# Another order of the same instructions in a fused attention and feed-forward kernel

## The chip, the cores and the metric

The kernel runs on one core of a Trainium2 chip. The metric is the time that the device takes for one execution, in microseconds (us); lower is better. A core has five engines with an instruction stream each: TensorE (PE, matrix products; its weight loads are shown apart as PEld), VectorE (DVE), ScalarE (ACT), GpSimd (POOL) and SyncE (SP), which here only issues transfers. Each engine takes its own instructions strictly in the order in which they stand, and waits at an instruction until the semaphores that it names have been raised by other engines or by transfers that have landed.

## What is computed

Attention of 8 batches x 8 heads over 576 queries of 64 elements, with keys and values averaged over groups of 8 (72 keys are left), and behind it a gated feed-forward layer on the 4608 tokens of 512 elements:

```python
k_p = k.reshape(B, H, Sp, pool, D).mean(axis=3)      # pool = 8, Sp = 72
v_p = v.reshape(B, H, Sp, pool, D).mean(axis=3)
scores = scale * np.matmul(q, k_p.transpose(0, 1, 3, 2))
attn = softmax(scores)                                # written out in the reference
x = np.matmul(attn, v_p)                              # as (4608, 512)
gate = 1.0 / (1.0 + np.exp(-(x @ w_gate)))            # w_gate, w_val: 512 x 1536
return (gate * (x @ w_val)) @ w_out                   # w_out: 1536 x 512
```

## The kernel before

**Tiles.** The 4608 tokens are nine blocks of 512. The first block is worked through by `first_pass` (L1147) in a hand-written list of steps, `ORDER` (L65). The other eight follow in four rounds of two blocks: `hidden_second` (L961) or `hidden` (L989) for the products with the gate and value weights, and `second_sums` (L1069) for those with the output weights. Between the products of a round stand the steps of the attention of the blocks that come next (`attention`, L722), as generators that are advanced a step at a time.

**Products.** A float32 product is made of three PE products of rounded numbers: every operand is split into a high part (a cast on ACT, `split`, L365) and the low rest (a subtraction on DVE). In the names, `hs` and `oparts` are such pairs of the hidden values and of the output weights, `parts` those of the gate and value weights, `xo` those of the attention's result. PE writes `chain` (gate and value products) and `acc` (output products), each in matmuls with 512 columns. For a pair of blocks the products are of sums and differences of quarters, seven in place of eight.

**Weights.** They arrive as 64-bit numbers and become float32 on the chip, in `to_f32` (L384): for each piece of 128x1024 elements two ACT instructions (`w<-raw` and `raw<-raw,cst`), one min/max and one shift-and-or on DVE or POOL, and behind these the split into parts. This falls into the first 150 us or so; later rounds read back the parts, which are kept in HBM (`kept...`). The rows call the loaded pieces `raw` (`raw64_...` and `raw_o_...` in the lists of instructions) and the converted ones `w` and `w_o`. The attention's steps show as `sc` (scores), `tp` and `tr` (transposes through PE), `av` (product with the values), `early`, `e`, `pm`, `ph`, `pl`, `r`, `rest`, `vres`, `vr`.

**What sets the order.** Nothing is issued while these functions run. Every engine call is taken down in a book (`Book`, `Taken`, `Engine`, L273 to L326), a group of matmuls as one unit, and at the end the units are issued in the order of a table:

```python
with tc.manual_schedule(engines={e.engine for e in engines}):
    for n in LATER.split() or range(len(book.units)):
        for taken in book.units[int(n)]:
            taken.issue(link)
```

`LATER` (L112 to L268) has 3801 numbers, one for each unit. So the table sets the order on every engine; which instruction waits for which follows from the data and the buffers. The call that is taken down is made in L317, which is why every row of the profile names that line. SP's transfers go round eight semaphores: the ninth is issued only when the first has landed, the tenth when the second has, and so on.

Of the kernel before, what the change touches and what calls it, by code (L numbers as in the profile page):

```python
# [112 lines left out]
5 4 3 6 0 10 2 7 24 13 17 19 20 8 26 12 27 18 16 30 9 22 21 75 25 34 36 35 46 32 1 44 39 54 38 40 11 29 47 28 51 15 31  # L113
65 52 66 37 61 57 41 67 62 42 14 60 63 53 73 82 45 74 70 87 79 71 97 136 84 123 77 112 109 111 80 88 100 99 101 96 98
59 83 104 91 105 89 81 106 72 130 78 107 110 93 92 95 94 58 114 127 115 116 119 125 86 103 120 128 197 144 122 143 142
135 141 85 137 138 129 157 205 140 147 145 121 102 204 134 132 153 154 152 133 155 151 131 222 90 108 139 118 161 203
164 149 124 162 148 216 126 163 156 167 150 166 189 170 158 169 174 159 165 146 171 190 160 55 168 177 179 243 172 173
117 178 56 193 180 186 230 181 223 182 199 244 233 201 196 206 200 202 209 185 184 33 188 225 192 49 191 176 195 240
175 236 183 187 234 226 247 239 238 250 245 251 259 217 248 257 282 253 242 258 212 279 283 64 276 252 232 261 286 267
237 43 269 211 278 50 256 274 219 268 254 218 277 266 265 231 275 272 241 280 221 299 288 298 284 228 305 227 229 285  # L120
289 292 113 302 290 281 293 255 235 273 294 303 316 300 246 326 332 329 304 333 335 301 311 287 318 331 330 328 327
317 334 307 308 306 198 309 314 352 322 260 312 315 325 362 324 353 208 364 291 345 323 366 339 313 346 348 338 365
349 321 340 296 399 350 360 310 215 376 68 342 405 361 341 297 358 343 214 344 69 367 347 295 263 382 355 373 370 337
264 374 380 224 375 270 271 377 336 371 386 387 356 385 354 395 357 372 398 396 397 393 411 392 403 402 48 207 368 391
400 412 363 417 406 410 407 369 419 378 404 409 401 388 418 416 389 408 414 413 424 426 320 447 319 425 23 423 381 427
422 262 379 446 429 420 384 434 421 383 194 444 430 220 457 437 435 431 578 466 436 483 441 485 443 452 449 451 492
210 428 469 470 467 468 464 461 493 462 213 463 450 432 433 497 486 500 390 440 487 415 501 448 438 456 584 471 484
472 480 498 481 477 490 439 458 473 517 482 502 249 478 479 460 521 513 465 474 491 475 499 530 454 453 531 590 488
532 527 476 510 522 489 524 528 394 525 445 523 685 529 504 526 507 495 540 546 496 516 545 505 459 519 506 514 494
455 511 534 442 544 533 542 512 503 577 541 551 548 520 582 535 556 518 549 557 558 76 596 567 560 568 570 571 536 569  # L130
611 564 543 603 574 572 550 580 606 581 351 565 515 555 566 561 554 612 562 539 573 604 576 607 632 563 605 597 600
579 598 552 583 608 538 601 537 602 599 648 622 623 559 642 629 553 627 669 359 678 636 575 628 672 953 659 656 675
588 591 679 613 585 633 586 676 667 660 593 595 594 589 680 666 587 592 673 614 677 609 670 610 621 508 674 615 630
# [1436 lines left out]
```

## Time and profile before

| what | us |
|---|---|
| three runs | 906.82, 908.58, 909.71 |
| their median | 908.58 |
| the profiled execution, its own time | 906.58 |
| span of its trace | 904.8 |
| PE busy | 891.4 |
| PE's weight loads busy | 732.7 |
| DVE busy | 657.4 |
| ACT busy | 544.5 |
| POOL busy | 200.0 |

The span is from the first to the last record of the profiled execution; 1.8 us of the own time lie outside of it. Busy times are sums over one engine. The granted clock of PE is at 1.00, that is the 2.4 GHz level, in every stretch that is shown.

### The profile page before, as it was taken

The numbers are of one execution on the slowest core, as the hardware profiler recorded it, in microseconds if no ns is written. First come the engines' busy times: TensorE is split into PE (matmuls) and PEld (weight loads), VectorE is DVE, ScalarE is ACT, GpSimd is POOL, SyncE is SP. The second block draws the span as 40 slices with busy tenths as digits, with TensorE's granted clock in tenths as the row PEclk, the third lists the DMA queues.
The fourth block names the chain that finished last, engine by engine and source line by source line (L and its number), as shares of the span: only waits on it lengthen the run. The fifth ranks groups of instructions, "written<-read, shape, count | busy, mean of one in ns | idle before, by whom it ended". The sixth has DMA issues, their size and how long they took to land.

```text
span 904.8 us, 12625 instructions
## 1 busy us (share of the span) xinstructions
PE 891.4 (99%) x4148; PEld 732.7 (81%) x4148; DVE 657.4 (73%) x1038; ACT 544.5 (60%) x1110; POOL 200.0 (22%) x369
## 2 busy tenths in 40 slices
PE   6999999999999999999999999999999999999998
PEld 5788878888888888888888888888888888888886
DVE  7989888889899999756668796355589552224863
ACT  5998998788978476545375555445365552224352
POOL 2422101012164235443443104132213000000000
PEclk9999999999999999999999999999999999999999
DMA  9899888889999888787987877676747776645554
GB/s 337 309 326 336 301 335 298 298 285 338 320 324 316 276 287 286 237 299 259 308 276 237 244 273 264 229 268 194 264 122 252 245 249 207 228 167 204 192 169 143
DMA packets 100433, 237.56 MB, mean 263 GB/s; under 512 B 13872, under 2 KB 34992, under 8 KB 98832
## 3 DMA queue, kind: packets, MB, share of 16 engines
q1 hardware_dynamic: 85328, 203.97, 66.6%
q0 software_dynamic: 15040, 32.79, 10.4%
q8 instruction: 33, 0.54, 0.2%
q14 instruction: 32, 0.26, 0.1%
HBM read 176.02 MB, written 60.69 MB: 262 GB/s over the span
## 4 chain that ended last, share of the span: by engine, by line
PE 81%; ACT 2%; DVE 1%; issue 0%; ACTq 0%
PE chain L317 50%; PE acc L317 25%; PE av L317 3%; PE sc L317 3%; ACT hs L317 0%; DVE s L317 0%; DVE hs L317 0%; PE tp L317 0%; DVE h L317 0%; ACT e L317 0%; ACT L317 0%; ACT raw_o L317 0%; DVE w_o L317 0%; ACT w_o L317 0%; ACT oparts L317 0%
## 5 line engine op out<-in xcount | busy, mean ns | idle before, releaser
L317 PE MATMUL chain<-xo,parts 128*128 128x512 f32 x2316 | 544.1, 392 | 0.5 <-ACT xs L317 0.5
L317 PEld LDWEIGHTS chain<-xo,parts 128*128 128x128 f32 x2316 | 430.7, 188 | 93.3 <-issue 1.0
L317 PE MATMUL acc<-hs,oparts 128*128 128x512 f32 x1008 | 237.0, 391 | 0.2 <-issue 0.2
L317 PEld LDWEIGHTS acc<-hs,oparts 128*128 128x128 f32 x1008 | 188.1, 188 | 40.6 <-DVE hs L317 1.2
L317 POOL DMA_DIRECT2D turned<-turn x240 | 131.7, 551 | 214.3 <-DVE turn L317 184.3
L317 DVE TENSOR_TENSOR y<-chain,sV 128x512 f32<-128x512 f32 x46 | 31.1, 686 | 69.6 <-PE chain L317 54.7
L317 ACT CAST hs<-h 128x1024 fp32r<-128x1024 f32 x52 | 54.3, 1051 | 27.2 <-PE acc L317 22.4
L317 DVE TENSOR_TENSOR hs<-h,hs 128x1024 fp32r<-128x1024 f32 x52 | 63.0, 1217 | 10.5 <-ACT hs L317 10.3
L317 ACT COPY chain<-chain 128x512 f32<-128x512 f32 x46 | 26.5, 577 | 52.8 <-PE chain L317 45.8
L317 DVE TENSOR_TENSOR y<-chain,sG 128x512 f32<-128x512 f32 x46 | 31.2, 682 | 34.2 <-PE chain L317 23.4
L317 ACT CAST hs<-s 128x1024 fp32r<-128x1024 f32 x36 | 37.5, 1050 | 28.5 <-DVE s L317 13.0
L317 DVE TENSOR_TENSOR hs<-s,hs 128x1024 fp32r<-128x1024 f32 x36 | 43.8, 1218 | 11.1 <-ACT hs L317 10.9
L317 ACT COPY sG<-chain 128x512 f32<-128x512 f32 x46 | 26.6, 584 | 41.0 <-PE chain L317 39.4
L317 ACT ACT_TABLE_LOAD x37 | 47.5, 1283 | 0.6
L317 ACT COPY sV<-chain 128x512 f32<-128x512 f32 x46 | 26.7, 584 | 34.0 <-PE chain L317 32.7
L317 ACT ACTIVATE gate<-chain 128x512 f32<-128x512 f32 x46 | 26.9, 594 | 31.8 <-PE chain L317 29.4
L317 DVE TENSOR_TENSOR h<-chain,gate 128x512 f32<-128x512 f32 x46 | 30.7, 679 | 20.1 <-PE chain L317 20.0
L317 PE MATMUL sc<-kbd,raw 128*128 128x144 f32 (+1 forms) x262 | 41.4, 297 | 0.3 <-ACT pr L317 0.2
L317 PEld LDWEIGHTS sc<-kbd,raw 128*128 128x128 f32 (+1 forms) x262 | 33.5, 176 | 8.6 <-issue 2.8
L317 ACT ACTIVATE gate<-y 128x512 f32<-128x512 f32 x46 | 28.9, 632 | 17.0 <-DVE y L317 16.8
L317 PE MATMUL acc<-oparts,hs 128*128 128x512 f32 x144 | 38.7, 402 | 0.0
L317 DVE TENSOR_REDUCE m<-sc 128x4 f32<-128x288 f32 x48 | 21.7, 452 | 17.5 <-PE sc L317 17.2
(210 smaller groups left out, 1099.9 us busy)
## 6 DMA issues: line engine op xcount, KB each, us to landing
oparts<-keptS SPq DMA_DIRECT2D x48, 512.0 KB, 4.7
oparts<-keptO SPq DMA_DIRECT2D x72, 256.0 KB, 4.7
raw<-in_wgv SPq DMA_DIRECT2D x12, 1024.0 KB, 8.1
out<-o SPq DMA_DIRECT2D x34, 256.0 KB, 3.8
raw<-in_kT SPq DMA_DIRECT2D x28, 288.0 KB, 5.0
raw<-in_qT SPq DMA_DIRECT2D x29, 256.0 KB, 4.9
raw<-in_vm SPq DMA_DIRECT2D x24, 256.0 KB, 5.5
raw_o<-in_wo SPq DMA_DIRECT2D x12, 512.0 KB, 8.5
```

Of the source, the lines that this page charges most:

```text
L317: return self._book.take(lambda: f(*args, **named))
```

## The change

`LATER` is replaced by another table with the same 3801 numbers, and nothing else. 3675 units stand at another place, by 16.7 places in the mean and by 245 at most. The 6909 instructions of the program are the same, one for one; on each of the five engines they come in another order.

```diff
--- before.py
+++ after.py
@@ -110,161 +110,161 @@
 LATER = """
-5 4 3 6 0 10 2 7 24 13 17 19 20 8 26 12 27 18 16 30 9 22 21 75 25 34 36 35 46 32 1 44 39 54 38 40 11 29 47 28 51 15 31
...
+5 3 4 0 10 6 2 17 7 13 19 24 8 20 12 16 26 27 9 30 36 1 75 18 34 46 35 40 21 22 29 39 47 38 54 25 28 44 65 32 31 52 66
...
```

The lists below give, for one engine and one place, the instructions in their order (engine line, operation, what is written and read, with the number of the buffer, and the size).

**The start.** SP before, from its second row on: `in_qT` and `in_kT` are queries and keys, `in_wgv` the gate and value weights (1 MB a load), `early_217<-in_qT` the queries of the fourth pair of heads.

```order
L317 DMA h_216<-in_qT 128x512
L317 DMA h_216<-in_kT 128x576
L317 DMA cst_84<-in_const 128x133
L317 DMA h_216<-in_qT 128x512
L317 DMA h_216<-in_kT 128x576
L317 DMA h_216<-in_qT 128x512
L317 DMA early_217<-in_qT 128x512
L317 DMA xs0_220<-in_sums8 128x360
L317 DMA xs0_220<-in_vn 64x512
L317 DMA raw64_237<-in_wgv 128x2048
```

SP now:

```order
L317 DMA h_216<-in_qT 128x512
L317 DMA h_216<-in_kT 128x576
L317 DMA cst_84<-in_const 128x133
L317 DMA h_216<-in_qT 128x512
L317 DMA h_216<-in_kT 128x576 x2
L317 DMA xs0_220<-in_vn 64x512
L317 DMA h_216<-in_qT 128x512
L317 DMA xs0_220<-in_sums8 128x360
L317 DMA raw64_237<-in_wgv 128x2048
L317 DMA early_217<-in_qT 128x512
```

The first load of queries has moved ahead of one of keys, and that of the fourth pair's queries behind the first load of weights; the first twelve loads are the same twelve.

DVE before, at about 20 us: `early_218<-early_217,early_218` and `r3_261` lead to the first block's attention result `xo1_268`; `raw_236` and `raw_234` are keys of the next block.

```order
L317 TENSOR_TENSOR early_218<-early_217,early_218 128x512
L317 CAST r3_261<-rest_260 128x4x32
L317 TENSOR_REDUCE early_218<-raw_236 128x72
L317 TENSOR_TENSOR early_218<-early_217,early_218 128x512
L317 TENSOR_TENSOR vres1_105<-vr_248,vres1_105 32x128
L317 TENSOR_TENSOR r3_261<-rest_260,r3_261 128x4x32
L317 SCALAR_TENSOR_TENSOR w4_249<-w4_249,raw64_237 128x1024
L317 TENSOR_TENSOR vres3_107<-vr_248,vres3_107 32x128
L317 CAST parts_259<-w4_249 128x2x256
L317 TENSOR_TENSOR xo1_268<-av_267,xo1_268 128x512
L317 TENSOR_TENSOR vres2_106<-vr_248,vres2_106 32x128
L317 CAST parts_262<-w4_249 128x2x256
```

DVE now:

```order
L317 TENSOR_TENSOR early_218<-early_217,early_218 128x512
L317 CAST r3_261<-rest_260 128x4x32
L317 TENSOR_TENSOR early_218<-early_217,early_218 128x512
L317 TENSOR_TENSOR r3_261<-rest_260,r3_261 128x4x32
L317 TENSOR_REDUCE early_218<-raw_236 128x72
L317 TENSOR_TENSOR vres0_104<-vr_248,vres0_104 32x128
L317 SCALAR_TENSOR_TENSOR w4_249<-w4_249,raw64_237 128x1024
L317 TENSOR_TENSOR vres2_106<-vr_248,vres2_106 32x128
L317 CAST parts_259<-w4_249 128x2x256
L317 TENSOR_TENSOR xo1_268<-av_267,xo1_268 128x512
L317 TENSOR_REDUCE early_218<-raw_234 128x72
L317 TENSOR_TENSOR xo1_268<-av_264,xo1_268 128x512
```

The reduction of `raw_236` has moved behind both steps of `early_218` and `r3_261`; that of `raw_234` stands between the two `xo1_268` now, and a cast of weights (`parts_262`) behind them.

**At about 74 us.** ACT before: `xs0_220<-av_330` is the copy that empties a PSUM bank of the attention; `raw64_...`, `w4_...` and `parts_...` belong to the conversion of weights.

```order
L317 CAST parts_329<-w4_319 128x2x256
L317 ACTIVATE raw64_257<-raw64_257,cst_84 128x1024
L317 ACT_TABLE_LOAD
L317 ACTIVATE y_331<-chain_326 128x512
L317 CAST parts_320<-w4_285 128x2x256
L317 ACTIVATE w4_342<-raw64_328 128x1024
L317 ACTIVATE raw64_328<-raw64_328,cst_84 128x1024
L317 COPY xs0_220<-av_330 128x512
```

ACT now:

```order
L317 ACT_TABLE_LOAD
L317 ACTIVATE y_331<-chain_326 128x512
L317 ACTIVATE raw64_257<-raw64_257,cst_84 128x1024
L317 COPY xs0_220<-av_330 128x512
L317 ACTIVATE w4_342<-raw64_328 128x1024
L317 CAST parts_320<-w4_285 128x2x256
L317 ACTIVATE raw64_328<-raw64_328,cst_84 128x1024
```

Between `y_331` and the copy of `av_330` there stood a cast and two conversion steps; now one conversion step stands there. In the same way, at about 123 us, ACT's order was two conversion steps, a table load, `y_390`, two casts and `y_388`; it is now the table load, `y_388`, two conversion steps and `y_390`, and the PE transposes there no longer have an ACT instruction to wait for.

**At about 80 to 87 us.** PE before, from the first output products of the first block on: `pl_227` is the low part of the attention weights.

```order
L317 MATMUL acc<-oparts,hs 128x512 x24
L317 MATMUL av<-early 128x64
L317 MATMUL av<-other,vres_106 128x64
L317 MATMUL av<-ph,vh_95 128x448
L317 MATMUL av<-pl,vh_95 128x448
```

PE now:

```order
L317 MATMUL acc<-oparts,hs 128x512 x23
L317 MATMUL tr<-identr,r_335 96x128 x4
L317 MATMUL acc<-oparts,hs 128x512
L317 MATMUL av<-ph,vh_95 128x448
L317 MATMUL av<-pl,vh_95 128x448
```

`av<-pl` follows the output products in both, with four transposes ahead of the last of these now. The first of the 24 that waits for the low part of `oparts_338` is the sixth before and the eighth now. DVE before, from the low part of `oparts_338` to the conversion of the next output weights `w_o_349`:

```order
L317 TENSOR_TENSOR oparts_338<-w_o_333,oparts_338 128x2x512
L317 TENSOR_TENSOR pl_227<-tp_343,ph_226 128x448
L317 TENSOR_TENSOR parts_348<-w4_342,parts_348 128x2x256
L317 TENSOR_REDUCE early_218<-raw_234 128x72
L317 TENSOR_TENSOR vl1_100<-early_218,vh1_95 64x64 x2
L317 TENSOR_TENSOR other_223<-early_218,other_223 32x64
L317 TENSOR_SCALAR w_o_349<-w_o_349 128x1024
L317 TENSOR_REDUCE early_218<-raws_228 128x64
L317 TENSOR_REDUCE early_218<-raw_231 96x64
L317 TENSOR_TENSOR h_216<-chain_339,y_352 128x512
L317 TENSOR_REDUCE early_218<-raw_235 128x72
L317 SCALAR_TENSOR_TENSOR w_o_349<-w_o_349,raw_o_337 128x1024
```

DVE now:

```order
L317 TENSOR_TENSOR oparts_338<-w_o_333,oparts_338 128x2x512
L317 TENSOR_REDUCE early_218<-early_218 96x64
L317 TENSOR_SCALAR w_o_349<-w_o_349 128x1024
L317 TENSOR_REDUCE early_218<-raw_234 128x72
L317 SCALAR_TENSOR_TENSOR w_o_349<-w_o_349,raw_o_337 128x1024
L317 TENSOR_REDUCE early_218<-raw_233 128x64
L317 TENSOR_TENSOR pl_227<-tp_343,ph_226 128x448
```

Two steps of the conversion of `w_o_349` and three reductions stand between `oparts_338` and `pl_227` now, where there was nothing.

## Rows read from the trace of the kernel before

**Rows 1.** The profile page: the span, the busy time of each engine with its share of the span and its instructions, and the shares of engines in the chain that ended last.

```profile
span 904.8 us, 12625 instructions
PE 891.4 (99%) x4148; PEld 732.7 (81%) x4148; DVE 657.4 (73%) x1038; ACT 544.5 (60%) x1110; POOL 200.0 (22%) x369
...
PE 81%; ACT 2%; DVE 1%; issue 0%; ACTq 0%
```

**Rows 2.** The view of waits for PE: what it waited for, us in total, times, longest.

```profile
PE sc L317 <- DMA h<-in_qT: 5.5, 1, 5.5
PE tp L317 <- DVE early L317: 0.9, 1, 0.9
PE tp L317 <- DVE r L317: 0.6, 1, 0.6
PE tp L317 <- ACT y L317: 0.5, 1, 0.5
PE chain L317 <- ACT xs L317: 0.5, 1, 0.5
PE sc L317 <- issue: 0.2, 1, 0.2
PE vr L317 <- DMA xs<-in_vn: 0.2, 1, 0.2
PE tr L317 <- ACT early L317: 0.2, 1, 0.2
PE sc L317 <- ACT pr L317: 0.2, 1, 0.2
PE acc L317 <- issue: 0.2, 1, 0.2
```

**Rows 3.** Windows of 20 us, three early and one late: length, then busy us (and instructions) of PE, PEld, DVE, ACT, POOL, the granted clock of PE, the busy share of the DMA engines and GB/s.

```profile
40.00:60.00 20.00, 20.00 (x105) 16.29 (x104) 18.57 (x34) 19.89 (x58) 3.15 (x6) 1.00 0.99 331
60.00:80.00 20.00, 19.50 (x99) 15.90 (x98) 17.02 (x31) 19.44 (x46) 3.09 (x3) 1.00 1.00 371
80.00:100.00 20.00, 20.00 (x98) 16.90 (x97) 17.66 (x27) 16.92 (x43) 5.05 (x9) 1.00 0.81 275
```

**Rows 4.** The same view, one window of the last round.

```profile
760.00:780.00 20.00, 20.00 (x89) 16.38 (x88) 5.16 (x8) 5.65 (x11) 0.00 (x0) 1.00 0.71 238
```

**Rows 5.** The chain of work that ended last, its end: start, us, what.

```profile
859.96 32.19 PE acc L317 x142
...
900.76 0.37 ACT o L317
```

**Rows 6.** The timeline from 0 to 28 us: start, us, engine, operation, count, and in brackets the idle time before and what ended it. SPq is the issue of transfers.

```profile
1.66 0.42 SPq L317 DMA_DIRECT2D h<-in_qT  x1
...
5.51 4.33 PE L317 MATMUL sc<-kbd,h 128*128 128x144 f32 x16 [5.51 <-DMA h<-in_qT]
...
12.43 1.60 PE L317 MATMUL sc<-kbd,early 128*128 128x144 f32 x8
...
13.62 0.34 SPq L317 DMA_DIRECT2D raws<-in_vr  x1
...
14.95 0.55 PE L317 MATMUL tp<-cst,early 128*128 128x128 f32 x3 [0.91 <-DVE early L317]
...
20.56 0.74 DVE L317 TENSOR_REDUCE early<-raw 128x72 f32<-128x576 f32 x1
...
20.66 0.63 PE L317 MATMUL tp<-cst,early 128*128 128x128 f32 x4 [0.56 <-DVE r L317]
...
27.52 4.85 PE L317 MATMUL chain<-xo,parts 128*128 128x512 f32 x20
```

**Rows 7.** The timeline at 74 us.

```profile
72.35 1.22 ACT L317 ACTIVATE raw<-raw,cst 128x1024 uint32<-128x1024 uint16 x1
...
73.48 0.56 ACT L317 COPY xs<-av 128x512 f32<-128x512 f32 x1
...
74.09 1.20 PE L317 MATMUL chain<-xo,parts 128*128 128x512 f32 x4 [0.50 <-ACT xs L317]
```

**Rows 8.** The timeline of PE at 123 us.

```profile
123.69 0.66 PE L317 MATMUL tp<-cst,early 128*128 128x128 f32 x4 [0.54 <-ACT y L317]
```

**Rows 9.** The timeline of PE from 80 us.

```profile
80.44 5.64 PE L317 MATMUL acc<-oparts,hs 128*128 128x512 f32 x24
...
86.45 0.37 PE L317 MATMUL av<-pl,vh 128*128 128x448 f32 x1
```

**Rows 10.** The timeline of DVE in the same stretch.

```profile
80.14 1.23 DVE L317 TENSOR_TENSOR oparts<-w_o,oparts 128x1024 fp32r<-128x1024 f32 x1
81.28 0.62 DVE L317 TENSOR_TENSOR pl<-tp,ph 128x448 fp32r<-128x448 f32 x1
...
82.42 0.74 DVE L317 TENSOR_REDUCE early<-raw 128x72 f32<-128x576 f32 x1
...
84.28 0.69 DVE L317 TENSOR_SCALAR w_o<-w_o 128x1024 f32<-128x1024 f32 x1 [0.38 <-ACT w_o L317]
84.89 0.68 DVE L317 TENSOR_REDUCE early<-raws 128x64 f32<-128x512 f32 x1
85.48 0.67 DVE L317 TENSOR_REDUCE early<-raw 96x64 f32<-96x512 f32 x1
...
87.33 1.21 DVE L317 SCALAR_TENSOR_TENSOR w_o<-w_o,raw_o 128x1024 uint32<-128x1024 uint32 x1
```

308 rows, old and new, of the table LATER are left out of this document.

## The prediction

> **What bounds the kernel now.** I read the page first, then the waits of PE, then windows, and last the timeline at the few places where PE waits. The page says that PE is busy 891.4 of 904.8 us and stands for 81% of the chain that ended last, where ACT has 2% and DVE 1% [rows 1]. PE's whole list of waits holds 9.2 us, and 5.5 of them are the wait for the first queries, before anything can run [rows 2]. After 12 us only small ones are left: 0.9 and 0.6 for DVE in the attention of the first block, 0.5 and 0.5 for ACT at 74 and 123 us, and some of 0.2. No wait for a transfer comes after 11.4 us. So an order can win little: the 13.4 us in which PE is idle, less 5.5 of first load and 0.4 of the last copy [rows 5], leave 7.5 us, of which the list names 3.7. It can lose much more, since every wait that it makes on PE is added to the time.
>
> Where it may lose shows in the windows. In the last round ACT and DVE are busy 5 to 6 of 20 us [rows 4]; between 40 and 100 us, where the weights are converted, ACT is busy 16.9 to 19.9, DVE 17.0 to 18.6, and the DMA engines up to 1.00 [rows 3]. There PE, ACT, DVE and the transfers are all near full, and whatever stands ahead of a copy or cast that PE needs can stop PE. The end is a plain run of output products, 142 in 32.19 us, which is 0.2267 us a matmul [rows 5]; I use this pitch below. The granted clock is 1.00, the 2.4 GHz level, in all these windows, so nothing is to be had from the clock.
>
> **The change part by part.** No instruction is added or removed, so all busy sums stay and only waits can change. I work against the profiled execution, 906.58 us; the median of the three runs is 908.58, that is 2.0 more, and the difference that the change makes is put onto the median at the end. The runs spread by 0.3%, and about 0.3% (2.7 us) is what a measurement of this kernel can tell from no change.
>
> *The start.* The load of queries that ends PE's first wait was SP's third, issued at 1.66 for 0.42 us [rows 6], and is now its second: PE begins 0.4 us sooner. The fourth pair's queries were ninth and are now twelfth, right behind a 1 MB load. Since the ring of eight lets the twentieth load go when the twelfth has landed, the twentieth row of SP (`raws<-in_vr`, issued at 13.62 [rows 6]) tells when the twelfth landed; the first twelve are the same twelve, so the queries now land near 13.6. PE took them at 12.43 without waiting, in 1.60 us [rows 6]. So PE stalls 1.2 us there and is done by 15.2, but its next step waited until 14.95 for DVE anyway, 0.91 us of it idle [rows 6]: some 0.3 us of the 1.2 is left over. If that cover is gone, all 1.2 are lost. On DVE a reduction of 0.74 us has moved from ahead of the two steps that lead to the first block's result to behind them; the wait of 0.56 us that ends at 20.66 beside it [rows 6] can go. In sum −0.4 + 0.3 − 0.6 = −0.7. Ends: −1.9 if all three idle pieces (0.4, 0.9, 0.6) go, +0.8 if the queries cost 1.2 in full and only the 0.4 is won. I take −0.7, since each of its terms has a row. What is won shows in the start of the first long chain, 27.52 now [rows 6].
>
> The Trainium skill (DMA: Bandwidth & Descriptors, Anatomy of one DMA) gives a transfer about 2.0 us and its bytes at 436 GB/s; it measured that on GpSimd's queue, and these are SP's. By it the queries would land near 7.0 + 2.0 + 3.0 = 12.0 us, an estimate, and PE would not stall: the start would be worth −1.0 and not −0.7. The trace disagrees with it (13.62), and I go by the trace.
>
> *At 74 us.* PE waited 0.50 us for the copy that empties a bank; the copy began at 73.48, as soon as a conversion step of 1.22 us was through [rows 7]. Both steps of that piece stand behind the copy now, and only one other step stands between the activation and the copy. The wait goes: −0.5. Next late is the cast of weights behind it, which moved back by one conversion step; it is part of the term on what comes back.
>
> *At 123 us.* PE's transposes waited 0.54 us for an ACT activation behind a table load and two conversion steps [rows 8]; this activation now stands ahead of the conversion: −0.5. The activation behind it takes over a later place, but its product is read by matmuls further on.
>
> *What comes back.* With ACT at 19.9 and 19.4 of 20 us [rows 3], PE runs as fast as ACT lets it in this stretch. A microsecond that is won ahead of it does not make ACT's work any shorter. I put half of the 1.7 us won down as lost again: +0.85. The bounds are 0 and +1.7.
>
> *A new tight place at 80 to 87 us.* Before, DVE made the low part of the attention weights (`pl`) right behind the low part of the output weights, at 81.28 for 0.62 us [rows 10], and PE read it at 86.45 [rows 9], with 4.5 us to spare. Now five steps stand between: 0.67 + 0.69 + 0.74 + 1.21 + 0.68 and the 0.62 of `pl` itself make 4.61 us by the rows of their kind [rows 10], and since each begins some 0.08 us before the one ahead has ended (1.14 from start to start for 1.23), it is about 4.1. On PE's side, from the matmul that waits for the output weights on, 17 of the 24 are left, 17 × 0.2267 = 3.85 us, and four transposes of a quarter of the columns, some 0.06 each: 4.1 as well. The spare time has gone from 4.5 to about nothing. DVE had 0.2 us in hand at the start of this stretch (the low part was through at 81.37, and the sixth matmul came at 80.44 + 5 × 0.2267 = 81.57), and has two more matmuls in hand now. The price lies between 0 and 1.0 (DVE a microsecond late); I take +0.3, nearer to the lower end, because of these two matmuls.
>
> *Elsewhere.* In the two orders I counted the matmul groups whose operand comes from an ACT or DVE instruction that itself waits for a matmul fewer than nine matmuls earlier (2 us): 77 before, 94 now. 17 more short leads, most of them after 300 us, where ACT and DVE have room [rows 4]: 0 taken, up to 17 × 0.2 = 3.4 us if each costs what the small waits cost [rows 2]. Against them stand the four waits of 0.2 us for ACT or for nothing named [rows 2], which may go: −0.8 at best, 0 taken.
>
> Sum: −0.7 − 1.0 + 0.85 + 0.3 = −0.55, that is 906.0 for the profiled execution and 908.0 on the scale of the median.
>
> **The rivals.**
>
> *Faster by more.* ACT and DVE do not hold PE back, and the short leads hold. Then the start gives 1.9, the two ACT waits 1.0 and the two waits of 0.2 for ACT 0.4: −3.3, 905.3. For it: at the four largest waits of today behind the first one, what PE waits for now stands earlier on its engine. Against it: the shares of ACT [rows 3], and the late queries.
>
> *Slower.* One mechanism: conversion steps, of 1.2 us each [rows 7, 10], stand right ahead of the cast or copy for which PE waits, as at 74 us before. The new order puts more of them there: at 80 to 87 us (+1.0), and at the 17 short leads, 0.2 each (+3.4); the late queries add 0.8, and the two waits that go give 1.0 back: +4.2, 912.8. It decides from about a dozen of the 17 on being late. For it: the full engines between 40 and 100 us. Against it: most of the new short leads lie where ACT is busy a third of the time.
>
> *PE has room that its busy share hides.* PE's weight loads are busy 732.7 us, 81% [rows 1]; if the other 172 us were gaps that an order can close, the time could fall as far as 734.5. But in the late window without any wait the loads are busy 16.38 of 20 us [rows 4], 82%: this is what they show when PE is full, and 732.7 / 16.38 × 20 = 894.6 us is the floor. I give it 1 in 100. The rule behind it is the Trainium skill's (Perfetto Trace Analysis, Identifying the Most-Contended Engine), which takes the matmul's busy share for a bad measure and wants that of the loads; here the trace shows that both are full together.
>
> *Nothing moves.* If the moves only swapped instructions that wait for the same thing, the waits would stay and the time be 908.6. The lists of all five engines differ, also at the places at which PE waits, so 1 in 100.
>
> **How the numbers follow.** The forecast (908.0) has 0.58, the faster rival 0.22, the slower one 0.18, the last two 0.01 each. Of the forecast's 0.58, with its terms between −0.3 and +3 at their ends, 0.05 falls below 905.9 (faster by 0.3%), 0.03 above 911.3 and 0.50 between. The faster rival's own time lies just beyond the line: 0.18 faster, 0.04 same. The slower one: 0.16 slower, 0.02 same. Together with the last two: faster 0.24, same 0.57, slower 0.19. The range goes down to 903.8, past the faster rival by the part of the named waits that would be left, and up to 912.0, which leaves out the upper half of the slower rival; some 0.17 is outside.
>
> **What would show it right or wrong.** In the profile after: PE's first wait at 5.1 instead of 5.5; a wait for the fourth pair's queries near 12 us (wrong if there is none); the wait of 0.6 at 20 us gone and the first long chain at about 26.8; no wait of PE for ACT at 74 and 123 us; at about 86 us none or a short one for `pl`. The busy sum of PE's loads stays at 733. The last run of output products keeps its 0.2267 us. The prediction is wrong if PE's list holds several new waits of 0.2 us or more between 40 and 600 us (slower), or if the chain of waits is PE alone from 27 us on with the start 1.9 us sooner (faster). A wait of PE for a transfer after 30 us would be something that none of these cases has.

## The result, and the profile after

The changed kernel takes 916.86 us (median of four runs, 914.67 to 917.82) against 907.80 (906.82 to 909.71) of the kernel before, four runs as well: 9.1 us more, ratio 1.0094, interval 1.0068 to 1.0120. It is slower by 0.9%, beyond what the runs scatter by, and above 912.0, the upper end of the range. The profiled execution took 916.85 us, 10.27 more than that of before, with a span of 915.1.

The page after: span, busy time of each engine, and the shares of the chain that ended last.

```profile
span 915.1 us, 12653 instructions
PE 899.4 (98%) x4148; PEld 736.8 (81%) x4148; DVE 656.4 (72%) x1038; ACT 543.9 (59%) x1110; POOL 203.4 (22%) x369
...
PE 74%; DVE 6%; ACT 5%; DMA 2%; issue 1%; DVEq 0%; ACTq 0%
```

Beside [rows 1] one sees at once that this is not a matter of waits alone. The same 4148 matmuls are busy 8.0 us longer and their loads 4.1; PE's idle time has grown by 2.3 only, from 13.4 to 15.7. POOL is busy 3.4 us longer with its same instructions; DVE and ACT are not. So matmuls ran slower somewhere, and something on GpSimd took longer.

PE's waits after, in the columns of [rows 2]:

```profile
PE sc L317 <- ACT kbd L317: 5.6, 2, 5.2
PE sc L317 <- POOL kbd L317: 1.9, 1, 1.9
PE acc L317 <- DMA oparts<-keptS: 1.1, 1, 1.1
PE sc L317 <- issue: 0.6, 1, 0.6
PE chain L317 <- ACT chain L317: 0.5, 1, 0.5
PE sc L317 <- ACT e L317: 0.4, 2, 0.2
```

The waits that the prediction meant to remove are shorter or gone: the first is 5.2 long and not 5.5, and of DVE at 15 and 20 us (0.9, 0.6) and ACT at 74 and 123 us (0.5, 0.5) nothing is left. In their place stand three of 0.4 to 0.6 in the first 16 us, one of 1.9 for GpSimd (`kbd`, the pooled keys that are put in place for the scores) and one of 1.1 for a transfer.

**Where the loss falls.** I laid the two traces over each other by the columns that PE had worked through (the columns of its matmuls, added up). The changed kernel is 3.4 us behind when the other is at 40 us, 2.9 at 80 us, 6.9 at 92, 7.5 at 116, 7.8 at 266, 9.4 at 345, and 10.3 from 700 us on. So there are three pieces: the start, a place at 90 us that costs 4.0, and small losses later, 2.5 of them after 266 us.

*The start.* The windows from 0 to the first long chain of products, after and then before (columns as in [rows 3]):

```profile
0.00:30.68 30.68, 24.06 (x103) 19.09 (x103) 21.95 (x51) 16.65 (x37) 8.57 (x27) 1.00 0.88 315
```

```profile
0.00:27.52 27.52, 19.99 (x103) 15.35 (x103) 21.96 (x50) 16.53 (x36) 7.57 (x27) 1.00 0.95 347
```

Both hold the same 103 matmuls. PE's idle time has shrunk, from 7.53 to 6.62; but the matmuls themselves took 4.07 us more. DVE and ACT did the same work in the same busy time. The granted clock's column says 1.00 in both windows and does not show it; the durations do:

```profile
5.17 2.26 PE L317 MATMUL sc<-kbd,h 128*128 128x144 f32 x8 [5.17 <-ACT kbd L317]
7.90 2.26 PE L317 MATMUL sc<-kbd,h 128*128 128x144 f32 x8 [0.47 <-ACT kbd L317]
10.55 2.26 PE L317 MATMUL sc<-kbd,h 128*128 128x144 f32 x8 [0.40 <-DMA h<-in_qT]
...
15.31 2.26 PE L317 MATMUL sc<-kbd,early 128*128 128x144 f32 x8 [0.56 <-issue]
...
18.43 2.61 PE L317 MATMUL vp<-early,xs 128*128 128x256 f32 x6
...
21.91 1.46 PE L317 MATMUL vp<-early,xs 128*128 128x256 f32 x6
...
30.68 1.66 PE L317 MATMUL chain<-xo,parts 128*128 128x512 f32 x6
```

The timeline of PE before has eight matmuls of the same kind here:

```profile
10.02 1.22 PE L317 MATMUL sc<-kbd,h 128*128 128x144 f32 x8 [0.18 <-issue]
```

Eight matmuls of 144 columns take 2.26 us each time up to 17 us in the changed kernel, and 1.22 at 10.02 us in the kernel before; six of 256 columns take 2.61 at 18 us but 1.46 at 22. From start to start the matmuls of 144 columns are 0.24 us apart at first and 0.12 later, and they are 0.24 apart again at 92.57 us (below), where the granted clock is near half. So PE's rate doubles at about 21 us here, and at about 10 us in the kernel before. The trace's own record of the granted clock begins only there, with 1.00 from 20.8 us here and from 9.9 us before; where it holds no record yet, the column shows 1.00 too. In the changed kernel the first long chain then begins 3.2 us later.

*The place at 90 us.* The timeline of all engines after:

```profile
88.20 0.60 DVE L317 TENSOR_TENSOR pl<-tp,ph 128x448 fp32r<-128x448 f32 x1
...
88.73 0.67 DVE L317 TENSOR_REDUCE early<-raws 128x64 f32<-128x512 f32 x1
...
88.96 3.56 POOL L317 TENSOR_SCALAR kbd<-early 64x72 f32<-64x72 f32 x1
...
89.27 0.37 PE L317 MATMUL av<-pl,vh 128*128 128x448 f32 x1
...
89.32 1.21 DVE L317 TENSOR_TENSOR hs<-h,hs 128x1024 fp32r<-128x1024 f32 x1
...
90.45 0.68 DVE L317 TENSOR_TENSOR parts<-w,parts 128x512 fp32r<-128x512 f32 x1
...
91.05 1.21 DVE L317 TENSOR_TENSOR oparts<-w_o,oparts 128x1024 fp32r<-128x1024 f32 x1
...
92.57 1.81 PE L317 MATMUL sc<-kbd,raws 128*128 128x144 f32 x6 [1.86 <-POOL kbd L317]
...
93.14 0.38 POOL L317 TENSOR_SCALAR kbd<-early 64x72 f32<-64x72 f32 x1
```

GpSimd's step of 64x72 elements takes 0.38 us at 93.14, and 3.56 at 88.96. It lasts until DVE has gone through three subtractions in a row, each of two operands in SBUF (89.32 to 92.26). PE is free at 90.7 and waits 1.86 us for it. In the kernel before, the same three stood at 90.03, 90.62 and 92.13 with a reduction of 0.45 us ahead of the last. The keys had been placed before that, two steps in 0.90 us, and PE took the scores at 87.07 without a wait:

```profile
83.25 0.90 POOL L317 TENSOR_SCALAR kbd<-early 64x72 f32<-64x72 f32 x2 [12.31 <-DVE early L317]
...
87.07 1.15 PE L317 MATMUL sc<-kbd,raws 128*128 128x144 f32 x8
```

Behind the wait in the changed kernel PE is also slow; the windows after:

```profile
92.00:94.00 2.00, 1.43 (x6) 1.43 (x7) 0.26 (x1) 0.00 (x0) 1.75 (x4) 0.61 0.98 365
94.00:96.00 2.00, 2.00 (x7) 1.64 (x7) 1.58 (x4) 0.00 (x0) 0.42 (x2) 0.54 1.01 410
96.00:98.00 2.00, 2.00 (x11) 1.61 (x10) 0.86 (x2) 0.00 (x0) 0.00 (x0) 1.00 1.03 420
```

The granted clock is 0.61 and 0.54, near the 1.2 GHz level, for the two windows after PE had stood still, and 1.00 again at 96. By these shares (0.39 + 0.46) × 2.0 = 1.7 us are lost on top of the 1.86, which makes 3.6 of the 4.0.

*Late.* The largest wait after 100 us is that for a transfer:

```profile
334.95 0.33 SPq L317 DMA_DIRECT2D oparts<-keptS  x1
...
343.75 2.55 PE L317 MATMUL acc<-hs,oparts 128*128 128x512 f32 x10 [1.05 <-DMA oparts<-keptS]
```

The parts of the output weights that PE needs there are read back by the load that SP issued at 334.95. It landed at 343.62, 8.7 us behind its issue, the longest of the 48 loads of its kind, whose median is 4.2. The other waits after 100 us add up to 1.5 us; all of those of the kernel before add up to 1.0 there.

### The profile page after: what moved, and what is told of

It is laid out like the page before. It is cut to its first block, busy times and chain, and to the rows that moved or that the text cites. A ratio compares the mean times of both kernels' runs of the same rounds, so it can differ in the third digit from the quotient of the medians.

```text
span 915.1 us, 12653 instructions
## 1 busy us (share of the span) xinstructions
PE 899.4 (98%) x4148; PEld 736.8 (81%) x4148; DVE 656.4 (72%) x1038; ACT 543.9 (59%) x1110; POOL 203.4 (22%) x369
## 4 chain that ended last, share of the span: by engine, by line
PE 74%; DVE 6%; ACT 5%; DMA 2%; issue 1%; DVEq 0%; ACTq 0%
PE chain L317 43%; PE acc L317 25%; PE av L317 3%; PE sc L317 3%; ACT e L317 1%; DVE h L317 1%; ACT L317 1%; DMA oparts<-keptS 1%; DMA h<-keptwV 1%; DVE parts L317 1%; DVE s L317 1%; ACT hs L317 1%; PE tp L317 0%; DVE early L317 0%; ACT xo L317 0%
## 5 line engine op out<-in xcount | busy, mean ns | idle before, releaser
L317 ACT CAST hs<-s 128x1024 fp32r<-128x1024 f32 x36 | 37.5, 1051 | 46.6 <-DVE s L317 26.8
```

The lines of the kernel that those rows point to most:

```text
L317: return self._book.take(lambda: f(*args, **named))
```

## The experiments

Two theories stood against each other for the largest piece. **Held by DVE**: the stall at 90 us and the slow matmuls behind it are one loss of 4 to 5 us, made by GpSimd's step that cannot go on beside DVE's subtractions. **Many small leads**: the short leads on ACT and DVE that the prediction counted add up, and the stall is only where they show. For the start, the order of the first transfers stood against the order of the engines' first steps.

**The order in pieces.** Four kernels take the table in one order up to a place and in the other behind it:

```diff
 start_of_after    LATER: changed up to place 156, earlier behind (to about 30 us)
 middle_of_after   LATER: earlier up to 156, changed to 735, earlier behind
 tail_of_after     LATER: earlier up to 735, changed behind (from about 125 us)
 head_of_after     LATER: changed up to 735, earlier behind
```

> The changed order up to the first product of the first block (156 units, some 30 us), the earlier order behind it. Theory (the start): in the changed order PE's first score products come in pieces with waits between them, and its matmuls stay at half their later rate until about 21 us where the earlier order has the full rate from 10 us on; this costs 3.5 us, so about 911.3 on the scale of the earlier median of 907.8, with the first long chain at about 30.7 us. Rival (the late conversions, as the prediction's slower case had it): the start costs at most 0.8, so 908.6 or less.

> The earlier order up to 30 us, the changed order from there to about 125 us, the earlier order behind it. Theory (one stall): PE waits some 2 us near 90 us for a GpSimd instruction (a block of keys placed into the score operand, 3.56 us long there) and then runs at half rate for 5 us; together 4 us, so about 911.8. Rival (many short waits for casts and copies behind conversion steps): 1.0 us at the tight place at 80 to 87 us less 1.0 for the two waits that are gone, so 907.5 to 908.8, with several waits of 0.2 us.

> The earlier order up to about 120 us, the changed order from there to the end. Theory (start and one stall hold most of the loss): the rest loses 2.5 to 3 us in small waits, the longest one of 1.1 us for a reload of output weights, so about 910.5. Rival (short leads make the loss): 3.4 us or more, 911.2 or above.

> The changed order up to about 125 us, the earlier order from there to the end. Theory: the start and the stall add up, 7.5 us, so about 915.3. Rival: the two hide each other in part (the later start gives the transfers and conversions of the middle time), so 912 to 913.5; or, by late conversions alone, at most 1.8, 909.6.

Measured against 907.86: the start alone 910.64 (1.0033, interval 1.0020 to 1.0045); the middle 921.48, the tail 919.00, the head 922.37. The last three are slower than the whole change, because of the seam: at place 735 the two orders have not converted the same weights, and PE stands still there for 8.0, 7.2 and 7.8 us. Their medians therefore say nothing on the change. Their traces do, up to the seam: with the earlier start, the stall comes again in the middle (1.87 us for `kbd`, GpSimd's step 3.58), and with the changed start it comes in the head. In the middle the granted clock stayed at 1.00 behind it, and in the head it fell to 0.68 and 0.50 in two windows of 2 us. So the stall does not need the changed start, and the fall of the clock may or may not follow it.

**The step moved to ACT.** One pair of keys is placed by ACT and not by GpSimd; the first kernel has the changed order, the second has the earlier one up to place 156.

```diff
         def place_keys(j, p):
...
-                if j:
+                if j and (j, p) != (2, 0):
                     nc.gpsimd.tensor_scalar_mul(out=t[r, c], in0=ks[j, p][r, :KEYS], scalar1=SCALE)
                 else:
                     nc.scalar.activation(t[r, c], ks[j, p][r, :KEYS], AF.Copy, scale=SCALE)
```

> The changed order, but the two steps that place the keys of the second later block's first pair of heads run on ACT instead of GpSimd, at the same places in the order. Theory (GpSimd held up by DVE): the wait of 2 us at 90 us is gone and with it the stretch at half rate behind it, so 3 to 4 us less than the changed order: 913 to 914. Rival (the keys come too late from DVE, or PE is short of something else there): the wait stays or another of 1 us or more takes its place, 915.5 or more.

> The earlier order up to 30 us, the changed order behind it, and the two steps of the keys on ACT. Theory (start and GpSimd's stall are most of the loss): 3 us for the start and 3.5 us for the stall come back, 910.0 to 910.5, and what is left over the earlier order are small waits after 130 us, 2 to 2.5 us. Rival (the loss is spread, and closing one wait opens another): 913 or more.

Measured: 911.97 (1.0052, interval 1.0033 to 1.0070), 4.9 less than the changed kernel, and 910.08 (1.0029, 1.0017 to 1.0041), 6.8 less. The timeline of the first:

```profile
80.57 5.63 POOL L317 TENSOR_SCALAR vres<-other,cst 96x64 fp32r<-96x64 f32 x2 [15.73 <-DVE other L317]
...
84.90 0.27 ACT L317 ACTIVATE kbd<-early 64x72 f32<-64x72 f32 x1
```

ACT places the keys in 0.27 us, and PE takes the scores at 88.67 without a wait. GpSimd is held as before, now at two other steps, of 3.75 and 1.90 us; the first of them lasts over two subtractions, a reduction and a min/max of DVE (80.55 to 84.09). PE's list of waits names neither. The stall is worth most of the 4.9, but not all: in this profile the matmuls of the start had come to the full rate at 12.0 us and the first long chain began at 28.94, against 30.68, so 1.7 of the 4.9 may be the start's, which leaves 3.2 for the stall. The 2.2 us that the second kernel leaves are neither start nor stall.

**The scores moved, GpSimd left as it is.** In three kernels PE, in the changed order otherwise, does products that are ready ahead of the scores that wait for the keys:

```diff
 products_first         LATER: units 519, 535 behind 512
 all_products_first     LATER: units 494, 519, 535, 577 behind 512
 scores_behind_products LATER: the same, and 533, 534 behind these
```

> The changed order with one group of score products (three instructions that wait for the keys from GpSimd at 90 us) moved behind twelve chain products, and DVE's reduction of it with it; GpSimd keeps its order and its slow instruction. Theory (PE only stood in line behind one late operand): the stall of 2 us and the half rate behind it go, 912.5 to 913.5, though GpSimd's instruction still takes 3 us or more. Rival (everything behind is as late, or the chain's own operands are not there yet): a stall of 1 us or more moves to the chain, 915.5.

> The changed order with both groups of score products that wait for the late keys at 90 us (four instructions' worth each) and DVE's two reductions of them behind the twelve chain products. Theory (PE stood in line behind one late operand): no wait for GpSimd on PE, 1.5 us or more of the 2 us stall gone and the rate stays full, 912 to 914; GpSimd's instruction still takes 3.5 us. Rival (everything behind is as late): a stall of 1 us or more on the chain's operands, 915 or more.

> As the run before with all products first, but GpSimd's two steps that overwrite the first block's keys stand behind the score products too (in the run before they stood ahead of them, so that one group of scores was computed from the wrong keys; its time is read as a time only). Theory (PE stood in line behind one late operand): 913 to 914, full rate throughout the 90s, GpSimd's instruction still 3.5 us. Rival: waits of 1 us or more on the chain's operands, 915 or more.

Measured: 915.23 (1.0089, 1.0074 to 1.0104), 913.35 (1.0071, 1.0052 to 1.0090) and 913.91 (1.0068, 1.0053 to 1.0083). In the second, one group of scores is computed from keys that the next ones have overwritten, so only its time is read. The first moved only one of the two groups that wait, and its wait stays at 1.87: no test. The third takes the wait away while GpSimd's step still lasts 3.56 us. It wins 3.0 us, near the 3.2 above, though its start is as slow as the changed kernel's (first long chain at 30.80) and 1.7 us come back as waits of a chain for DVE and ACT (0.9 and 0.8). It is PE's waiting that costs, then, and not GpSimd's lateness in itself.

**What holds GpSimd.** Behind the last product, four steps of 64x72 on GpSimd beside rows of one kind on DVE (the added code lengthens the run, so only its trace counts):

```diff
+        for work_of, times in ((None, 0), (two_from_sbuf, 6), (one_reduced, 8), (one_from_psum, 10), (one_clipped, 10)):
+            nc.vector.tensor_copy(kbd[0][:D, :KEYS], ta[:D, :KEYS])
+            for _ in range(times):
+                work_of()
+            for i in range(1, 5):
+                nc.gpsimd.tensor_scalar_mul(out=kbd[i][:D, :KEYS], in0=kbd[0][:D, :KEYS], scalar1=SCALE)
```

> The earlier order, and behind the work of the kernel five groups: a small copy on DVE, then a row of DVE instructions of one kind, and beside it four GpSimd instructions of the kind that placed the keys (64x72). The kinds: none; subtraction of two operands in SBUF (128x1024), six; sum over groups of eight (one operand), eight; product with one operand in PSUM (128x512), ten; clip to a range (one operand, 128x1024), ten. The result is the reference's; the groups add some 30 us. Theory (GpSimd waits while DVE works on two operands in SBUF): the four take 0.4 us each alone and beside the one-operand kinds, and the first of the four lasts until the row of subtractions is through, 5 us or more. Rival (GpSimd is slowed by every kind of DVE work alike, or by none): the four are about as long in all groups with DVE work.

```profile
901.93 1.76 POOL L318 TENSOR_SCALAR kbd<-kbd 64x72 f32<-64x72 f32 x4 [193.77 <-DVE kbd L318]
...
903.83 7.51 DVE L318 TENSOR_TENSOR bench<-bench 128x1024 f32<-128x1024 f32 x6
903.99 5.07 POOL L318 TENSOR_SCALAR kbd<-kbd 64x72 f32<-64x72 f32 x4 [0.31 <-DVE kbd L318]
...
911.52 1.76 POOL L318 TENSOR_SCALAR kbd<-kbd 64x72 f32<-64x72 f32 x4 [2.46 <-DVE kbd L318]
...
921.55 1.76 POOL L318 TENSOR_SCALAR kbd<-kbd 64x72 f32<-64x72 f32 x4 [8.27 <-DVE kbd L318]
...
928.66 7.48 DVE L318 TENSOR_SCALAR bench<-bench 128x1024 f32<-128x1024 f32 x10
928.80 3.15 POOL L318 TENSOR_SCALAR kbd<-kbd 64x72 f32<-64x72 f32 x4 [5.49 <-DVE kbd L318]
```

Alone, beside reductions and beside products with an operand in PSUM the four take 1.76 us. Beside subtractions with two operands in SBUF they take 5.07, about one subtraction (1.25) for each, and beside clips of one operand 3.15, about one clip (0.75) for each.

A second bench asked whether it matters that DVE's row is unbroken. Its steps write to different places, so that none waits for the one ahead, and it has a group of four half-size subtractions:

```diff
+        outs = [t[:, h:h + 1024] for t in (to, tp, tq) for h in (0, 1024)]
...
+        for o in outs[:4]:
+            nc.vector.tensor_tensor(out=o[:, :512], in0=ta[:, :512], in1=tb[:, :512], op=ALU.subtract)
```

> The earlier order, and behind its work four groups: four GpSimd instructions (64x72) beside six DVE subtractions of two SBUF operands that write to six different places, so that none waits for the one ahead; the same beside six sums; then one GpSimd instruction on 128x1024 beside four DVE subtractions (128x512), and beside four sums. The result is the reference's. Theory (GpSimd gets its turn only where DVE has a break; in the first measurement every subtraction waited for the one ahead, and one GpSimd instruction came through at each): the first of the four small ones lasts until the six subtractions are through, 6 to 7 us, and the four take 0.44 each beside the sums; a subtraction beside the long GpSimd instruction takes 1.5 instead of 0.68, a sum no longer than alone. Rival (one GpSimd instruction between any two of DVE): 1.2 us each, 5 us for four, as before, and the 3.56 us in the kernel have another cause.

```profile
901.68 7.08 DVE L318 TENSOR_TENSOR bench<-bench 128x1024 f32<-128x1024 f32 x6
901.79 4.91 POOL L318 TENSOR_SCALAR kbd<-kbd 64x72 f32<-64x72 f32 x4 [193.12 <-DVE kbd L318]
...
915.65 2.48 DVE L318 TENSOR_TENSOR bench<-bench 128x512 f32<-128x512 f32 x4
915.81 2.57 POOL L318 TENSOR_SCALAR kbd<-kbd 64x72 f32<-64x72 f32 x1 [5.09 <-DVE kbd L318]
```

Beside 128x1024 steps GpSimd again gets one step in for each of DVE's. Beside the four of 128x512 a single step lasts to the end of the row, as it does at 90 us. The theory that it is always held to the end of a row falls. The size of DVE's steps alone does not decide it either, since the row at 90 us holds two of 128x1024. What decides between one instruction and the row stays open.

**The start.** Loads and engines' steps in either order, both with the keys on ACT, and some products of zeros ahead of all else:

```diff
 old_loads_keys_on_act   changed order; SP's first 12 loads in the earlier order
 new_loads_old_start     earlier order up to place 156; SP's first 12 loads in the changed one
```

```diff
+    warm = ps.tile([P, 2 * KEYS], F32, name="warm", tag=CHAIN[5])
+    for _ in range(8):                       # 7 in before_early_matmuls
+        nc.tensor.matmul(warm, lhsT=kbd[4][:, :P], rhs=kbd[4], start=True, stop=True)
     book.open = True
```

> The changed order with the keys on ACT, and the first twelve loads in their earlier order; PE, DVE, ACT and GpSimd keep the changed order. Theory (the loads' order breaks PE's first products apart): the first score products run in one piece again, PE has its full rate by 10 to 12 us in the profile, the first long chain starts at 27.7 instead of 28.9 to 31, and the time is 1 to 2 us less than with the changed loads, 910 to 911 against 911.97. Rival (DVE's and PE's order): 28.6 or later and 911.9.

> The earlier order up to 30 us but with the first twelve loads in the changed order, the changed order behind it, keys on ACT: the counterpart of the run with only the loads put back. Theory (at the start it is the order of PE, DVE and ACT that costs, not that of the loads): 910.1, as with the earlier loads (910.08). Rival (the loads cost): 911.5 or more, with PE waiting 1 us or more for the fourth pair's queries near 13 us.

> The changed order with eight more matmuls on PE (zeros times zeros, results never read) in the 4 us in which it waits for the first loads. Theory (half of the loss at the start is PE's rate): the first score products already run at the full rate, the first long chain starts at 28.5 to 29 instead of 30.7, and the time is 2 us less than the changed order: 914.9. Rival (the loss at the start is the late transfers and DVE's order alone): the first long chain stays at 30 or later and the time at 916.9.

> The earlier order with seven more matmuls (zeros, never read) on PE while it waits for the first loads. Theory (PE's first products run at half rate until it has worked for some time; DVE waits for them): the first score products at full rate, the first long chain some 0.5 to 1 us sooner than 27.5, 907.0 on the scale of 907.6. Rival (DVE or the keys bind there, or the rate falls again in the next break): 907.6 or more, first long chain at 27.3 or later.

Measured: the earlier loads with the changed steps 912.44 (1.0057, 1.0042 to 1.0071); the changed loads with the earlier steps 911.87 (1.0050, 1.0035 to 1.0065). With both changed it was 911.97 and with neither 910.08: either half of the change alone costs the start 1.8 to 2.4 us, and together they cost no more. Neither theory of the start is right alone. In the one profile DVE's `pm` lasts 1.53 us beside a step of GpSimd and the granted clock is at 0.50 from 17.4 to 20.8 us; in the other PE waits 2.07 for keys and the clock is at 0.50 from 11.7 to 18.5.

The kept traces say more on the start than the medians. Eight have the earlier first steps and loads: their rate doubles at 9.7 to 11.3 us, and the first long chain begins at 27.25 to 28.23, in the median at 27.55. Seven have the changed ones. Where the rate had doubled by 12 us and stayed (`head_of_after`, `keys_on_act`), the chain begins at 28.63 and 28.94; where it doubled at 20.8 to 21.4 us (the changed kernel, `scores_behind_products`, `start_of_after`), at 30.68 to 31.15; the other two (`products_first`, `all_products_first`) lie between, at 29.27 and 29.32. So the changed first steps cost 1.1 to 1.4 us at the full rate and 3.1 to 3.6 with the late one; no run isolates what makes it late. At the full rate PE has these waits, in the timeline of PE of `head_of_after`:

```profile
13.99 1.22 PE L318 MATMUL sc<-kbd,early 128*128 128x144 f32 x8 [1.38 <-DMA early<-in_qT]
...
16.59 0.33 PE L318 MATMUL tp<-cst,pm 128*128 128x128 f32 x1 [0.90 <-DVE pm L318]
...
21.86 0.52 PE L318 MATMUL tp<-cst,early 128*128 128x128 f32 x3 [0.77 <-DVE r L318]
```

The zero products in the changed order give 912.53 (1.0058, 1.0040 to 1.0076), 4.3 less than without, but not as meant: the rate rose at 7.6 us, was back at half from 11.0 to 17.8, and the first long chain began at 29.46, 1.2 earlier. The stall lasted 1.8 as before, until 91.3 us, but the granted clock stayed at 1.00 behind it, and the wait for the read-back was gone. So it tells little on the start. In the kernel before they give 907.10 (0.9991, 0.9981 to 1.0000), not to be told from none; there the rate doubled at 9.9 us with them as without, and the first long chain began at 28.22, so what was to be tried did not come about.

**The two ACT waits alone.** In the kernel before, only the units that the prediction named at 74 and 123 us are moved:

```diff
 LATER, the earlier order:
+unit 441 (the copy `xs`) ahead of 457
+unit 732 (the activation) ahead of 743
```

> The earlier order with two ACT instructions moved as the change moved them: the copy that empties a bank at 74 us ahead of two conversion steps, and the activation at 123 us ahead of the conversion steps and the table load behind it. Theory (these waits were real and cost what the trace says): both waits of 0.5 go, 1.0 to 1.3 us less, 906.5 against 907.8. Rival (ACT is full there, so that the gain is lost again within 20 us): 907.5 or more.

Measured: 907.76 against 907.84, ratio 1.0000 (0.9990 to 1.0009), which leaves room for a gain of 0.9 us at most. At 74 us PE no longer waits for the copy, and soon after for something else:

```profile
75.80 0.66 PE L317 MATMUL tp<-cst,early 128*128 128x128 f32 x4 [0.70 <-DVE h L317]
```

The transposes of [rows 8] begin at 123.69 in this trace too, behind a wait of 0.18 and not 0.54, so by then nothing of either gain is left in it.

**The late part.** The earlier order up to place 1200 (about 175 us), the changed one behind:

> The earlier order up to some 175 us, where all weights have been converted, and the changed order behind it. Theory (small waits in the later part, the longest one of 1.1 us for a reload of output weights at 344 us): 2 to 2.5 us over the earlier order, 910. Rival (start and stall make all of it): 907.8 to 908.5.

Measured: 912.61 (1.0054, 1.0039 to 1.0069), six runs from 910.09 to 913.66. It has a seam too, with a wait of 1.5 us at 218 us that the changed order by itself has at 0.2. Less that, the late loss is 5.2 − 1.3 = 3.9 by the median, and 3.5 − 1.3 = 2.2 by its profiled execution (910.09 against 906.58); two of its six runs lie at 910.1 and four at 912.0 to 913.7. The wait for the read-back is there again, 0.7 long.

## Why the prediction was wrong

**The step that failed** is the sentence that all busy sums stay and only waits can change. An instruction was priced by its row in the trace of before, wherever it was moved. Two durations did not stay: that of GpSimd's step, by what DVE did beside it (0.38 or 3.56 us), and that of PE's matmuls, by the rate that PE had at the time (0.12 or 0.24 us for 144 columns). By the experiments the stall at 90 us with what follows it costs 3.0 (scores moved) to 4.9 (keys moved, of which 1.7 may be the start's), the start 1.9 (911.97 − 910.08) to 2.8 (910.64 − 907.86), and the rest 2.2 (910.08 − 907.84): 7.1 to 9.9, against 9.1. By the one trace the start has 3.4, the stretch from there to 116 us 4.1, and the rest 2.8. The two accounts differ by when the start's rate doubled, which was at 21 us in this execution and at 9 to 21 in others of the same first steps.

The trace of before held a warning, in the view of the tile `kbd` (count, then the shortest, median and longest time in ns): GpSimd's sixteen steps of this size took 0.38 to 1.48 us there.

```profile
L317 POOL TENSOR_SCALAR kbd<-early x16: 381/387/1476, 21.5 to 100.5; 64x72 f32<-64x72 f32 x16
```

Term by term:

- *GpSimd's queue* is in no term and in no rival. GpSimd is busy 22% and is not among PE's waits [rows 1, 2], and the order of DVE's steps was looked at for DVE's readers only. That cost 3.0 to 4.9. The Trainium skill (SBUF — State Buffer, SBUF: two separate sides) says that a DVE instruction with two SBUF inputs and a GpSimd instruction that reads SBUF exclude each other, and that the later one is blocked for the whole of the other. The trace agrees with the exclusion (3.56 against 0.38; four steps 5.07 beside such subtractions, and 1.76 beside reductions or with an operand in PSUM), but in it one step was held by three instructions and not by one.
- *The clock.* "Nothing is to be had from the clock" failed. The column reads 1.00 over the start of before too, but sixteen matmuls in 4.33 us [rows 6] and eight of the same kind in 1.22 behind them show that the first 10 us ran at half rate, so the 2.4 GHz level does not hold for every stretch of [rows 6]. It matters when the half rate ends.
- *The start*, −0.7 predicted, −1.9 to +0.8 as its ends: measured +1.9 to +2.8. The first matmul came at 5.17, 0.34 sooner. The late queries landed where the twentieth load said: in `head_of_after`, where PE was at full rate, it waited 1.38 for them until 13.99. In the changed kernel PE came later and took them at 15.31. The waits for DVE at 15 and 20 us went from its list by that lateness, and not by DVE's new order: at the full rate PE waits again, 0.90 for `pm` and 0.77 for `r` in `head_of_after`, 0.89 and 0.78 in `keys_on_act`, where the prediction gave 0.6 for the second as won. The first long chain came at 30.68 and not at 26.8.
- *At 74 and 123 us*: both waits went, as predicted. Half of what was won was put down as lost again, with all of it as the bound. The kernel with the two moves alone is 0.1 faster, its interval allows 0.9, and by its trace nothing was left at 123 us; so half is not excluded, and all lost is the likelier.
- *The tight place at 80 to 87 us*, +0.3: `pl` was done at 88.80 and read at 89.27 without a wait, so 0. The danger in the same row of DVE was the one of GpSimd, a microsecond later.
- *Elsewhere*, 0 taken and 3.4 as the end: about 2.2. This term was mis-sized and its bound held, in part by luck: its largest wait, 1.05 for a read-back, is not of the short leads on ACT and DVE that the bound was made of. The others are 0.5 for ACT and several of 0.2.
- *The rivals.* Slower it was, but not by the mechanism that this rival named: conversions ahead of casts on ACT and DVE show in the late small waits at most. A transfer that PE waits for after 30 us, which none of the cases had, is there (1.05 at 343.75). The busy sum of PE's loads, 733 and taken for fixed, is 736.8.
- *A sum.* The list of waits in [rows 2] adds up to 9.0 and not 9.2, so it names 3.5 of the 7.5 us and not 3.7; nothing else rests on it.

What stays open: why the same short standstill lowered the granted clock in the changed kernel and in `head_of_after`, but not in `middle_of_after`, nor in two other kernels (`early_matmuls`, `products_first`); why the rate of the changed start doubles at 9 us in some executions and at 21 in others; and why either half of the changed start costs as much as the whole. No version was faster than the kernel before by more than the runs scatter.

## What to carry to other kernels

When instructions are only moved, ask of each engine's moved work what will run beside it at the new place: a small GpSimd step that PE needs should not stand beside a row of DVE steps with two SBUF operands, and ACT can take it in 0.27 us. Compare busy sums of the same instructions first: PE's 8.0 and POOL's 3.4 more pointed at both causes before any wait was read. A wait of PE that is removed where the other engines are full may give nothing that can be measured (0.1 us of 1.0 here), and one that is added may cost twice its length (3.6 us for 1.86). A duration read from a trace holds for the place at which it was read: look at the spread of all instructions of its kind before it is taken for fixed.

## What was not expected of the hardware

- Four 64x72 steps on GpSimd took 1.76 us alone, 5.07 beside two-operand subtractions and 3.15 beside clips of one operand; a single one lasted 2.57 beside four 128x512 subtractions and 3.56 in the kernel. It goes the other way too: DVE's `pm` of 128x512 took 1.52 us beside a GpSimd step of 128x1024, instead of 0.68; the row is DVE's timeline of the changed order with the keys on ACT:

```profile
15.31 1.52 DVE L317 TENSOR_TENSOR pm<-e,early 128x512 f32<-128x512 f32 x1
```

- The column of the granted clock stood at 1.00 over the start while matmuls were spaced at twice their later distance; there the spacing is the measure.
- After 1.8 to 1.9 us without work PE ran for 3 to 4 us at the 1.2 GHz level in two traces (0.61 and 0.54 in the windows above) and stayed at 1.00 in three others.
